# One engine for each bank of top-k candidates, constants loaded as listed work, and another order of the whole program

## The chip, the core and the metric

The kernel runs on one core of a Trainium2 chip. The core has a matmul engine (TensorE, PE in the profile, with its weight loads as PEld), a vector engine (VectorE, DVE), an activation engine (ScalarE, ACT), a general engine (GpSimd, POOL) and a queue engine (SyncE, SP), which here issues nearly all DMAs. Each engine works through its own list of instructions in order and waits on semaphores where it needs another's result. The metric is device time of one execution in microseconds (us); lower is better. Before the change the median of 3 runs is 329.95 us (326.61 to 335.99).

## What is computed

There are 4 batches of 12608 tokens of width 128, and 49 agents for each. The agents attend to the keys, which gives 49 agent values; every token's query then attends to the agents. On the result `x`, the 128 tokens of each batch with the highest gate score go through a two-layer network and are added back.

```python
a2k = softmax(scale * agents @ k.T)
agent_v = a2k @ v
x = softmax(scale * q @ agents.T) @ agent_v
scores = x @ w_gate
top = the 128 rows of each batch with the highest scores
out = x.copy()
out[top] += sigmoid(scores[top]) * (relu(x[top] @ w1) @ w2)
```

## The kernel before

A batch's tokens lie on 128 partitions in 99 columns, cut into 7 chunks (six of 15 columns, one of 9). For a batch the work has these steps, and the names in quotes are those of the work list.

- Keys: per chunk a load of 0.98 MB, two score products on PE ("S15", L343, 8 matmul instructions each), two turns on DVE (L349) and two maxima (L356). When all chunks are through, the maximum per agent is spread to all partitions ("mT", "mB", L385, and "mb", L388).
- Values: per chunk POOL subtracts the maximum ("X15", L398), ACT takes the exponential ("E15", L401), and PE multiplies with the chunk of v ("av", L413, two instructions for each column). After the last chunk the sums are gathered ("pw", L430) and scaled, and split in two half-precision parts, the weights `ws`.
- Queries: per chunk scores, maximum, subtraction (POOL, L485), exponential, split in two halves (L497, L498) and turns on PE ("fT", L513) with a copy out by DVE or ACT (L516).
- Gate scores ("pg", L537), then the reciprocal sums ("rates", L551 to L555).
- Results: for groups of up to 4 columns the products with `ws` ("po", L583, two instructions for each column), then an eviction that scales by the rates, on DVE in one instruction (L596) or on ACT in one for each column (L599), and a store of the chunk by SP (L604).
- Top-k (`topk`, L609): each partition's 8 best scores (L618) are spread by PE over two banks of PSUM, 4 candidates for each partition and bank ("all", L625). Every one of a partition's 8 candidates is compared with all 512 values of both banks, 16 comparisons of 512 columns for a batch. On each bank DVE does four (L633) and ACT does four (L638); the sums land in the tile `cnt` of that bank. Counts, places and indices follow on one more bank ("pc" L645, "at" L665, "p1" L672 to L675, "x8" L680, "pr" L681, "idx" L685 to L692).
- Experts: a gather of the chosen rows by POOL (L722), the attention of these rows again, the two layers (L810, L832) and a scatter (L840), for batches 0 to 2 together and for batch 3 alone.

The order is not left to the loops. `Work.op` only lists each piece of work with what it reads and writes; `Work.issue` (L209) then takes the 1302 pieces in the order of the table `ORDER` (L108), three characters each, the last bit of which says on which of two engines a piece runs (evictions, copies and relu have the choice). So a row of `ORDER` sets every engine's list, and SP's. Loads and result tiles share 8 buffers ("in"), scores share 28 ("s"), and the general PSUM banks are 6 ("b").

The reads and writes that a piece lists bound where the table may put it. The waits between engines are set below that, from the tiles and PSUM banks that instructions touch. A piece that compares a candidate lists the bank as read and its own column of `cnt` as written.

Three small loads stand outside the list, at the program's start, on ACT's queue: the agents, the constants `cst` (293 KB) and the gate weights (64 KB). `cst` is first read by "pw" of the first batch, apart from a conversion on DVE ("tri", L304).

Of the kernel before, what the change touches and what calls it, by code (L numbers as in the profile page):

```python
# [27 lines left out]
A = 49  # L28
# [12 lines left out]
ONACT = (4, 4, 4, 4)  # L41
# [5 lines left out]
TOP = 8  # L47
# [5 lines left out]
def const_layout(capacity):  # L53
    nst = max(1, -(-capacity // P))
    parts = {
        "sel": (2 * A),
        "steps": ROUNDS * (CANDS + 1),
        "offs": ROUNDS * CANDS,
        "jv": COLS,
        "slot": nst,  # L60
        "prow": 1,
        "tri": P,
        "srow": nst * P,
        "pcol": 1,
        "kk": TOP,
        "under": TOP * len(ONACT),
    }
# [4 lines left out]
    return at, pos, nst


def make_consts(capacity):
# [38 lines left out]
    "03001c09g05u09i0aw09k18216c15c0om0ra03q0361840aq0by0c003203405w16e16g01405y0601nw1ny08a03g03c04q0460oo15i"
    "09q09s0as1o00os0ou1o21o40480rc0re1860bu06204003e0rg15e04g03w16i0000oq0ri0ow04a04k18804i04s03y04u08c03m03o"
    "1o61o81oa0rk18a15k0bx18c0640661oc06815g15m03803a03i03k03s03u04204404c04e04m04o04w04y05019s1oi19y0520541a0"
    "1oe06a1og0s606c1ol0sc05606e05805a0rm15o0oy0ro08e0rq0rs05c0s806h0sa19u19w0se0pi05e0du0dx0pk0po0pm0pq1l615q"
    "05g1l81lc09m1le1a209o0fo0e20ps0qe0dg0dy0fr15s0e10do0di0dq1la0io0jg0ju0qk0qg0qi0fc0fe06i16k1a407o0ry0ru18e"
    "0s00p00sg0qm0e408g08m0iq0iu0rw08o1a60ji0iw0jm0jk0jw0jo0e60e90is0qo0j00iy0k00jy0k20k80ia0j20km0ea18w1pm15u"
    "08i08k0kg0js0jq0k40k60si0pu0pw0p20py09u15w0d80dc1601620p40kk0ki08q0df0sk0c40ii0im0j40j80ik0ja0jc0ku0kw0je"  # L120
    "08s0ka0ky0j60ic0fg15y0qq0q00fj07m0ko0fk0qs0fn16m0sm0ke0ie0ig0pa0pd0ks0p60p90l00le0fs14g0dk06k0q20b00l20c2"
    "1ps0l40kq0kc0l61pu0l80q60ay0d60so0sq0q51a80dn09w0su0da1po1pq1aa0lk0lu0me0mo0sw0qu19218y19019414m14o0ss0eg"
    "0ek0ej0ec0ef0ey1lg0en0f214i17417a0la0f51ag14k17c1961760fy1781pw17e0f00gq0gs1ai14q0mi0lo0lc0lw0lm0mg16o0m4"
    "0m61py1q016q0qw0ly0lg0li0lq0ls0m014s1980m80ms0ds0n20m216s16w0eu0mq0q816u0ex0g21ac0qy0g41ae0r116y0eo0eq19a"
    "10617g18g0ma0mc0mk0mm0my1li0n017i0mu0mw0n40n619c18i0g11lk19e0n80f60r20na0r50gc0f90gf0zs10e0g619k0g90nc0ne"
    "0ng0ni0nk0zu1qi1081qo1qq0zy0nm1lm14u19m0no1lo10c10g0tw0ok0pe1001021040zw10i10a18k0qa18o0r60pg0r80sy0s20tu"
    "0es0z00oi0z21qk0t00z41qm0z610k11c0ze10y0fa14w18q18m0fu0s40qc10s19g1lu0ty19i1lw0fx11k1qs10u10m0zm0gk0gn0zg"
    "0z811o10w10q11m0zo10o0zq0za0zc1qu14y1161500ua0x20u01qw0ud0x50zi1180zk11a11011e1540ue1m21m817k1520uh17m11g"
# [926 lines left out]
```

## Time and profile before

| | |
|---|---|
| median of 3 runs | 329.95 us (326.61 to 335.99) |
| the profiled execution | 330.46 us, its span 328.7 us |
| mean granted TensorE clock | 0.926 |
| busy: PE, DVE, ACT, POOL | 280.5, 218.2, 192.5, 143.3 us |
| moved by DMA | 106.70 MB, mean 325 GB/s |

The span runs from the first to the last instruction of the profiled execution, and its time lies 1.8 us above it. Busy time is a sum over the span, and the stages differ much: the first 50 us and the last 90 us do not look like the 150 us between. Matmuls overlap in PE's pipeline, and their ends are modelled, so that a fully busy PE isn't one at its peak; its clock is granted at one of two levels, 1.0 (2.4 GHz) or 0.5 (1.2 GHz) in the tables.

### The profile page before, as it was taken

What the parts mean: (1) busy time and instruction counts of PE and PEld (TensorE: products, weight loads), DVE (VectorE), ACT (ScalarE), POOL (GpSimd) and SP (SyncE); (2) the same over time, 40 slices, a digit from 0 to 9 for tenths busy, and PEclk for the clock granted to TensorE, in tenths of its full rate; (3) what the DMA queues carried; (4) which work ended last, traced back from release to release, by engine and by line L of the source; (5) the groups of instructions that cost most, each with busy time, mean ns of one, the idle gap of its engine ahead of it and who ended that gap; (6) DMA issues with size and microseconds to landing.
All of it is one profiled execution on the core that took longest, in us unless ns stands there. A gap on an engine that the chain in (4) does not pass through costs nothing. (4 is left out here: it accounts for less than half of the span.)

```text
span 328.7 us, 8664 instructions
## 1 busy us (share of the span) xinstructions
PE 280.5 (85%) x3524; PEld 194.7 (59%) x3524; DVE 218.2 (66%) x499; ACT 192.5 (59%) x446; POOL 143.3 (44%) x110
## 2 busy tenths in 40 slices
PE   0977868999999979999999798988466999599991
PEld 0322323496545647966356695656455999498791
DVE  0599995896799847069868748684096556577530
ACT  1063743725667638965487755865905567789540
POOL 0269488948835494941229640009505110001022
PEclk9999997999999979999999999999958556969997
DMA  8999999898998997999899999989793305655692
GB/s 282 425 426 416 425 420 406 346 422 352 370 342 330 378 421 251 348 410 417 291 352 367 381 310 395 383 328 403 271 394 134 129 10 197 252 242 224 278 381 78
DMA packets 18589, 106.70 MB, mean 325 GB/s; under 512 B 2544, under 2 KB 3824, under 8 KB 18544
## 3 DMA queue, kind: packets, MB, share of 16 engines
q1 hardware_dynamic: 17472, 105.07, 81.7%
q8 instruction: 30, 0.49, 0.6%
q0 software_dynamic: 256, 0.52, 0.5%
q10 hardware_dynamic: 816, 0.50, 0.5%
q14 instruction: 15, 0.12, 0.1%
HBM read 79.87 MB, written 26.21 MB: 323 GB/s over the span
## 5 line engine op out<-in xcount | busy, mean ns | idle before, releaser
L343 PE MATMUL b<-in,ag_sb 128*32 128x480 f32 (+1 forms) x896 | 100.2, 568 | 18.8 <-DMA in<-qT 10.2
L349 DVE STREAM_TRANSPOSE s<-b 128x480 f32<-128x480 f32 (+1 forms) x112 | 69.2, 635 | 27.3 <-PE b L343 26.1
L583 PE MATMUL b<-ws,s 98*128 98x128 f16 x792 | 66.1, 243 | 9.9 <-DVE in L596 8.0
L583 PEld LDWEIGHTS <-s 98*128 98x128 f16 x792 | 57.6, 111 | 24.3 <-issue 23.2
L343 PEld LDWEIGHTS b<-in,ag_sb 128*32 128x32 f32 x896 | 24.7, 112 | 62.6 <-issue 28.0
L599 ACT ACTIVATE in<-b,r 128x128 f32<-128x128 f32 x182 | 50.8, 403 | 17.1 <-PE b L583 10.8
L485 POOL TENSOR_TENSOR s<-s,qm 128x735 f32<-128x735 f32 (+1 forms) x28 | 37.9, 1369 | 46.5 <-DVE qm L483 33.0
L398 POOL TENSOR_TENSOR s<-s,mb 128x735 f32<-128x735 f32 (+1 forms) x28 | 46.7, 1700 | 25.2 <-DVE mb L388 25.2
L498 POOL TENSOR_TENSOR f<-s,f 128x735 f16<-128x735 f32 (+1 forms) x28 | 40.9, 1473 | 36.4 <-issue 21.6
L516 ACT COPY s<-b 98x1024 f16<-98x1024 f16 (+2 forms) x42 | 37.8, 918 | 30.4 <-PE b L513 29.1
L413 PE MATMUL v<-in,s 128*64 128x129 f32 x792 | 48.4, 279 | 3.6 <-DMA in<-va 2.4
L413 PEld LDWEIGHTS v<-in,s 128*64 128x64 f32 x792 | 45.6, 139 | 6.1 <-issue 3.5
L487 ACT ACTIVATE s<-s,lift 128x735 f32<-128x735 f32 (+1 forms) x28 | 24.5, 884 | 27.3 <-POOL s L485 27.2
L633 DVE SCALAR_TENSOR_TENSOR ge<-b,top,minus 128x512 bf16<-128x512 f32 x32 | 23.9, 746 | 24.4 <-ACT ga L638 22.9
L513 PEld LDWEIGHTS <-f 128*98 128x98 f16 x396 | 27.4, 133 | 17.5 <-issue 14.1
L513 PE MATMUL b<-idh,f 128*98 128x128 f16 x396 | 32.9, 232 | 2.4 <-DVE s L349 0.9
L356 DVE TENSOR_REDUCE mx<-b 128x1 f32<-128x480 f32 (+1 forms) x56 | 32.8, 606 | 2.3 <-PE b L343 0.9
L497 ACT CAST f<-s 128x735 f16<-128x735 f32 (+1 forms) x28 | 21.6, 786 | 13.2 <-POOL s L494 11.5
L638 ACT ACTIVATE ga<-b,top 128x512 bf16<-128x512 f32 x32 | 22.1, 691 | 10.0 <-DVE ge L633 8.2
L483 DVE TENSOR_REDUCE qm<-s 128x15 f32<-128x735 f32 (+1 forms) x28 | 23.5, 852 | 0.2
L401 ACT ACTIVATE s<-s 128x735 f32<-128x735 f32 (+1 forms) x28 | 21.0, 790 | 1.7 <-POOL s L398 1.7
L722 POOL DMA_INDIRECT xq<-q,idx x4 | 4.0, 1000 | 38.1 <-DVE idx L692 37.3
(132 smaller groups left out, 246.2 us busy)
## 6 DMA issues: line engine op xcount, KB each, us to landing
in<-va SPq DMA_DIRECT2D x24, 967.5 KB, 8.9
in<-qT SPq DMA_DIRECT2D x24, 960.0 KB, 10.0
in<-kT SPq DMA_DIRECT2D x24, 960.0 KB, 9.4
out<-in SPq DMA_DIRECT2D x24, 960.0 KB, 7.7
in<-va SPq DMA_DIRECT2D x4, 580.5 KB, 9.1
in<-qT SPq DMA_DIRECT2D x4, 576.0 KB, 7.2
in<-kT SPq DMA_DIRECT2D x4, 576.0 KB, 7.0
out<-in SPq DMA_DIRECT2D x4, 576.0 KB, 8.3
```

The costliest lines, as they stand in the source:

```text
L343: nc.tensor.matmul(ps()[32 * i:32 * i + 32, :w], ag_sb[:, b, 32 * h:32 * h + 32], x()[:, w * i:w * i + w], start=True, stop=True,)
L349: nc.vector.transpose(s()[:, :n, 32 * h:32 * h + 32], ps()[:, :w].rearrange("p (t c) -> p t c", c=32))
L356: op("V", f"M{n}", lambda _, h=h, ps=ps: nc.vector.tensor_reduce(top[:, c, h:h + 1], ps()[:, :w], axis=AX.X, op=ALU.max), r=[ps], w=[(f"mx ...
L398: op("G", f"X{n}", lambda _, sv=sv, n=n: nc.gpsimd.tensor_tensor(sv(), sv(), d["mb"].unsqueeze(1).broadcast_to([P, n, A]), op=ALU.subtract ...
L413: nc.tensor.matmul(av()[o:o + AP_, :C + 1], s()[:, t], x3[:, t], start=(j < 2), stop=(j >= COLS - 2))
L485: op("G", f"qx{n}", lambda _: nc.gpsimd.tensor_tensor(sv(), sv(), wide, op=ALU.subtract), r=[f"qm{b}{c}"], w=[s])
L487: op("A", f"qe{n}", lambda _: nc.scalar.activation(sv(), sv(), AF.Exp, scale=SCALE, bias=lift), w=[s])
L498: op("G", f"ql{n}", lambda _: nc.gpsimd.tensor_tensor(f()[:, :n, A:], sv(), f()[:, :n, :A], op=ALU.subtract), r=[s, (f, 0)], w=[(f, 1)])
L513: nc.tensor.transpose(wide_pt()[:R, P * (t - lo):P * (t - lo) + P], f()[:, t, :], idh)
L516: (nc.vector.tensor_copy if e == "V" else nc.scalar.copy)(flat(ft()).bitcast(F16)[:R, P * lo:P * hi], wide_pt()[:R, :P * (hi - lo)])
L583: nc.tensor.matmul(p3()[:, t - lo], d["tile", c](t), ws[:, b, i, :C], start=(i == 0), stop=(i == 1))
L599: nc.scalar.activation(o4[:, t - lo], p3()[:, t - lo], AF.Copy, scale=d["r"][:, j0 + t:j0 + t + 1])
```

## The change

On the first bank of candidates DVE now does all 8 comparisons, on the second ACT all 8; before it was 4 and 4 on both. The threshold `under` loses its per-batch columns. The copy "x8" goes from ACT into DVE's "p1". The loads of `cst` and of the gate weights become pieces of the list, on SP, with the reads of them listed. And the whole table `ORDER` is another one, with 1300 pieces.

```diff
-ONACT = (4, 4, 4, 4)
...
-        "under": TOP * len(ONACT),
+        "under": TOP,
...
-    under = np.full((len(ONACT), TOP), capacity - 0.25, np.float32)
-    for b, n in enumerate(ONACT):
-        under[b, TOP - n:] -= 512.0
-    c[:, slice(*at["under"])] = under.reshape(1, -1)
+    c[:, slice(*at["under"])] = capacity - 0.25 - 256.0
...
-    "0c60nq0nw0ny0ns0nu0o00o20cc0t20t80ta0t40t60tc0te0tg0o40c80ca0ce0cg08u0900920ci0ck0ti08w0o606m06s06u06o06q"
+    "0ca0cc0cg0ce0ci0t40t60ck0cm0co0cq0cs0cu0t80cw0cy0d00ns0nu0ny0ta0nw0o00tc0te0tg0ti0tk0tm0a20a80oo0ou0ow0aa"
...
-    nc.scalar.dma_start(cst, consts)
     wg_sb = own("wg_sb", [P, C])
-    nc.scalar.dma_start(wg_sb, wgb)
+    op("S", "dma308", lambda _: nc.sync.dma_start(cst, consts), w=["cst"])
+    op("S", "dma66", lambda _: nc.sync.dma_start(wg_sb, wgb), w=["wg"])
...
-        side8 = TOP - ONACT[b]
...
             for k in range(TOP):
-                if k < side8:
+                if h == 0:
                     op("V", "ge", lambda _, h=h, k=k, bk=bk: nc.vector.scalar_tensor_tensor(
...
         def marks(_):
             nc.vector.tensor_copy(bs, at())
+            nc.vector.tensor_copy(x[:, TOP:TOP + 1], at()[:, 0:1])
...
-        op("V", "p1", marks, r=[pc], w=[f"p1{b}", f"fl{b}"])
-        op("A", "x8", lambda _: nc.scalar.copy(x[:, TOP:TOP + 1], at()[:, 0:1]), r=[pc], w=[(f"x{b}", 1)])
+        op("V", "p1", marks, r=[pc], w=[f"p1{b}", f"fl{b}", (f"x{b}", 1)])
```

What the two tables make of the engines' lists is shown at two places. The first is the stretch behind the last batch's key maximum, where the comparisons of batches 1 and 2 stand before, and those of batch 2 after. In a row, `c11` is the sum tile of bank 1 of batch 1 (`c02`: bank 0 of batch 2), the `b` behind the arrow is the PSUM bank that is read, and a wait names the engine whose semaphore is waited on. DVE before, from the last batch's `mb` on:

```order
L388 COPY mb3_236<-b4_107 128x49 [waits PE_49]
L633 SCALAR_TENSOR_TENSOR ge_147,c02_224<-b0_103,top2_222,minus2_133 128x512
L516 COPY s9_81<-b5_108 98x1024 [waits PE_49]
L349 STREAM_TRANSPOSE s25_97<-b2_105 128x15x32 [waits PE_49]
L633 SCALAR_TENSOR_TENSOR ge_147,c02_224<-b0_103,top2_222,minus2_133 128x512 [waits DVE_49]
L349 STREAM_TRANSPOSE s25_97<-b4_107 128x15x32 [waits PE_49]
L596 TENSOR_TENSOR in0_64<-b5_108,r1_194 128x384 [waits DMAHW0_49,PE_49]
L633 SCALAR_TENSOR_TENSOR ge_147,c11_198<-b2_105,top1_195,minus2_133 128x512 [waits DVE_49,PE_49,Activation_49]
L633 SCALAR_TENSOR_TENSOR ge_147,c01_197<-b3_106,top1_195,minus2_133 128x512 [waits DVE_49,Activation_49]
L633 SCALAR_TENSOR_TENSOR ge_147,c02_224<-b0_103,top2_222,minus2_133 128x512 [waits DVE_49]
L596 TENSOR_TENSOR in0_64<-b5_108,r1_194 128x512 [waits DMAHW6_49,PE_49]
```

and ACT before, in the same stretch (L401 are the exponentials "E15" of the last batch):

```order
L638 ACTIVATE ga_148,c11_198<-b2_105,top1_195 128x512 [waits Activation_49]
L401 ACTIVATE s23_95<-s23_95 128x15x49 [waits Pool_49]
L680 CAST x0_172<-b1_104 128x1
L638 ACTIVATE ga_148,c12_225<-b4_107,top2_222 128x512 [waits DVE_49,PE_49,Activation_49]
L638 ACTIVATE ga_148,c11_198<-b2_105,top1_195 128x512 [waits Activation_49]
L638 ACTIVATE ga_148,c02_224<-b0_103,top2_222 128x512 [waits Activation_49]
L401 ACTIVATE s14_86<-s14_86 128x15x49 [waits Pool_49]
L401 ACTIVATE s10_82<-s10_82 128x15x49 [waits Pool_49]
L401 ACTIVATE s6_78<-s6_78 128x15x49 [waits Pool_49]
L638 ACTIVATE ga_148,c11_198<-b2_105,top1_195 128x512 [waits Activation_49]
L401 ACTIVATE s5_77<-s5_77 128x9x49 [waits Pool_49]
```

DVE's comparisons on `c11` and `c01` wait for ACT, which in its turn has comparisons on the same two tiles spread between the exponentials; three DVE rows behind the first of them stands an eviction of results (L596). DVE after, behind the same `mb`:

```order
L628 SCALAR_TENSOR_TENSOR ge_145,c02_222<-b1_104,top2_220,minus2_131 128x512
L680 SCALAR_TENSOR_TENSOR e21_201<-b3_106,cst_115 128x1 [waits PE_49]
L683 SCALAR_TENSOR_TENSOR e21_201<-cst_115,e21_201,b3_106 128x8 [waits DVE_49]
L687 SCALAR_TENSOR_TENSOR idx1_202<-b3_106,e21_201 128x1 [waits DVE_49]
L628 SCALAR_TENSOR_TENSOR ge_145,c02_222<-b1_104,top2_220,minus2_131 128x512
L628 SCALAR_TENSOR_TENSOR ge_145,c02_222<-b1_104,top2_220,minus2_131 128x512 [waits DVE_49] x2
L592 TENSOR_TENSOR in2_66<-b4_107,r2_219 128x128 [waits DMAHW4_49,DMAHW1_49,PE_49]
L628 SCALAR_TENSOR_TENSOR ge_145,c02_222<-b1_104,top2_220,minus2_131 128x512 [waits DVE_49] x2
L614 MAX_INDEX at82_221<-top2_220,scs_142 128x8
L479 TENSOR_REDUCE qm_3_4_243<-s17_89 128x15
L628 SCALAR_TENSOR_TENSOR ge_145,c02_222<-b1_104,top2_220,minus2_131 128x512 [waits DVE_49]
L592 TENSOR_TENSOR in1_65<-b2_105,r2_219 128x512 [waits DMAHW6_49,PE_49]
```

and ACT after:

```order
L397 ACTIVATE s0_72<-s0_72 128x15x49 [waits Pool_49]
L397 ACTIVATE s7_79<-s7_79 128x15x49 [waits Pool_49]
L633 ACTIVATE ga_146,c12_223<-b5_108,top2_220 128x512 [waits DVE_49,PE_49]
L633 ACTIVATE ga_146,c12_223<-b5_108,top2_220 128x512 [waits Activation_49] x2
L397 ACTIVATE s16_88<-s16_88 128x15x49 [waits Pool_49]
L633 ACTIVATE ga_146,c12_223<-b5_108,top2_220 128x512 [waits Activation_49]
L397 ACTIVATE s23_95<-s23_95 128x15x49 [waits Pool_49]
L633 ACTIVATE ga_146,c12_223<-b5_108,top2_220 128x512 [waits Activation_49] x4
L648 COPY b1_104<-cst_115 128x128 [waits DVE_49,PE_49]
```

There each tile (`c02`, `c12`) is on one engine alone, and no comparison waits for the other engine but the first of ACT's, which also waits for PE's spread; the comparisons of batches 0 and 1 have left this stretch for earlier ones.

The second place is the start. ACT before, its first five rows:

```order
L265 DMA ag_sb_113<-agT 128x4x64
L267 DMA cst_115<-consts 128x586
L269 DMA wg_sb_117<-wgb 128x128
L487 ACT_TABLE_LOAD
L487 ACTIVATE s1_73<-s1_73,lift_129 128x9x49 [waits Pool_49]
```

ACT after:

```order
L261 DMA ag_sb_113<-agT 128x4x64
L483 ACT_TABLE_LOAD
L483 ACTIVATE s0_72<-s0_72,lift_127 128x9x49 [waits Pool_49]
L487 ACTIVATE qm_0_6_164<-qm_0_6_164,eps_129 128x9 [waits DVE_49]
L493 CAST f0_100<-s0_72 128x9x49 [waits Pool_49]
```

The load of the constants has left ACT's queue. It stands in SP's list behind the loads of batch 0's values, 40 rows in, and SP issues it when the loads ahead have their buffers:

```order
L326 DMA in6_70<-va 128x1935 [waits DMAHW7_49,PE_49]
L326 DMA in7_71<-qT 128x1920 [waits PE_49]
L264 DMA cst_115<-consts 128x562 [waits DMAHW0_49]
L326 DMA in0_64<-qT 128x1920 [waits DMAHW1_49,PE_49]
L326 DMA in4_68<-qT 128x1920 [waits DMAHW2_49,PE_49]
```

The pieces of choice are split otherwise too: evictions of results are 39 on DVE and 69 on ACT before, 48 and 60 after; copies of turned tiles ("fT") are 14 and 42 before, 20 and 36 after. The two large loads of expert weights (0.46 MB each) stand right behind the last load of values before; after, `w1` stands behind three stores of results that follow those values, and `w2` behind six.

## Rows read from the trace of the kernel before

**Rows 1.** The page, the granted clock in 40 slices of the span.

```profile
PEclk9999997999999979999999999999958556969997
```

**Rows 2.** Busy time by stage: start and end, length, engines (instructions), clock, DMA.

```profile
0.00:51.00 51.00, 34.11 (x321) 12.03 (x321) 38.77 (x75) 20.26 (x30) 28.60 (x28) 1.00 0.98 400
51.00:76.70 25.70, 25.70 (x334) 16.75 (x334) 17.94 (x28) 11.31 (x15) 20.42 (x14) 0.93 0.98 391
76.70:221.90 145.20, 136.10 (x1913) 88.97 (x1909) 104.88 (x224) 97.53 (x193) 70.09 (x50) 0.99 0.94 356
221.90:254.80 32.90, 21.64 (x283) 18.77 (x282) 18.04 (x49) 17.84 (x43) 16.11 (x10) 0.87 0.79 299
254.80:300.70 45.90, 41.92 (x502) 40.45 (x503) 28.32 (x91) 33.92 (x125) 3.25 (x4) 0.69 0.40 159
300.70:328.70 28.00, 21.03 (x179) 17.72 (x178) 10.26 (x33) 11.62 (x42) 4.87 (x5) 0.93 0.66 265
```

**Rows 3.** Waits: engine and line, waited for: total us, times, longest.

```profile
DVE ge L633 <- ACT ga L638: 22.9, 8, 11.1
ACT ga L638 <- DVE ge L633: 8.2, 5, 3.5
```

**Rows 4.** Timeline from 221 us: start, length, engine, work, [idle before <-releaser].

```profile
221.89 0.43 PE L385 MATMUL b<-dg,ones_f 2*128 2x64 f32 x2
...
222.65 11.64 POOL L398 TENSOR_TENSOR s<-s,mb 128x735 f32<-128x735 f32 x7 [21.40 <-DVE mb L388]
...
228.53 3.53 PE L413 MATMUL v<-in,s 128*64 128x129 f32 x60 [1.02 <-ACT s L401]
...
237.34 0.75 DVE L633 SCALAR_TENSOR_TENSOR ge<-b,top,minus 128x512 bf16<-128x512 f32 x1 [11.07 <-ACT ga L638]
...
240.68 1.01 PE L583 MATMUL b<-ws,s 98*128 98x128 f16 x8 [6.48 <-DVE in L596]
...
253.36 0.17 PE L681 MATMUL b<-x,p 128*128 128x10 bf16 x1 [2.63 <-DVE flags L675]
...
254.83 0.75 PE L430 MATMUL b<-avs,cst 128*98 128x129 f32 x2 [0.43 <-DVE e L685]
```

**Rows 5.** Windows as in rows 2, first and last of four in a row.

```profile
254.00:260.00 6.00, 5.57 (x45) 5.24 (x43) 3.72 (x16) 3.95 (x14) 0.00 (x0) 0.50 0.28 110
...
272.00:275.00 3.00, 3.00 (x27) 3.00 (x26) 2.79 (x10) 2.90 (x12) 0.00 (x0) 0.50 0.09 22
```

**Rows 6.** Timeline, PE's work in short bursts at full clock.

```profile
200.89 1.82 PE L343 MATMUL b<-in,ag_sb 128*32 128x480 f32 x16 [0.82 <-DMA in<-kT]
...
203.46 0.94 PE L537 MATMUL x<-ws,s 98*128 98x3 f16 x30
...
204.25 0.63 PE L513 MATMUL b<-idh,f 128*98 128x128 f16 x8
...
208.36 1.08 PE L583 MATMUL b<-ws,s 98*128 98x128 f16 x16
...
218.81 1.14 PE L625 MATMUL b<-idf,top 128*128 128x128 f32 x8
...
303.97 1.45 PE L810 MATMUL b<-xT,s 128*128 128x384 f32 x4
```

**Rows 7.** Timeline, the end of the last batch's top-k.

```profile
283.13 0.75 DVE L633 SCALAR_TENSOR_TENSOR ge<-b,top,minus 128x512 bf16<-128x512 f32 x1 [4.59 <-ACT ga L638]
...
300.36 0.33 ACT L680 CAST x<-b 128x1 bf16<-128x1 f32 x1
...
300.74 0.17 PE L681 MATMUL b<-x,p 128*128 128x10 bf16 x1
```

**Rows 8.** Groups of instructions by line and form: count, busy us, mean ns.

```profile
L596 DVE TENSOR_TENSOR in<-b,r 128x512 f32<-128x512 f32 x22 | 14.9, 684 | 1.5 <-PE b L583 1.3
```

**Rows 9.** Timeline, the start.

```profile
8.02 12.29 PE L343 MATMUL b<-in,ag_sb 128*32 128x480 f32 x104 [8.02 <-DMA in<-qT]
```

**Rows 10.** DMA issues: bytes, us from issue to landing.

```profile
cst<-consts ACTq DMA_DIRECT2D x1, 293.0 KB, 7.5
```

More of the change, by code (lines that the diff above doesn't have):

```diff
@@ L114 @@
[L114 to L128, printed above, removed]
@@ new lines @@
+    "0ao00k15c08007w0bm0700bo0bq08207y00s00m07200u15i15e0rq09c0rs0ru0740p20p408400o15k0bs00q07600w15g09e15m05m"
+    "0s00rw05o0d60bu0ry0d80s20p60qu09g0bw00y05q0100pc01201401605s05u0p80by0c101a07807a05w0aq0c20pe0q00pa0as01c"
+    "01k0240ji02601e01m01o01i0180jq01g0c509i01q02i0060au0ay0js02a0ju01s01y0qw0b002802k02o02m02q01w02u01u02c022"
+    "05y0q207c0aw07e08607g0qy15o15q0j40s802002e07i00e02g00i00g07m00800c0sa0q809k07o09m00a02w02y0300sc0se032034"
+    "09o0880360qa02s07l08a0sg04u0021680iq16a0r00q40r416e16c0si06008c0iy0is16g0r316i0j215s15u03g03q08e0iu08g0sk"
@@ new lines @@
+    "03a0jw0380r609u0j609w0ko03k0ka0ic15w15z06206403i09q03c03e0iw0660j00q70kq0jy0k20ku0k40k80jk0ja09s0680kw0l0"
+    "0j803m03o0jc0ky0jo0ks0jg0k60jm0je0ie0kc0ki0ik0ii0io0kg0km0l20ke0k00kk03u04404e04y04o18000003s0sm04a04004c"
+    "08i0so0sq0sw04203w03y04604804g0ig0sy1600l408k16k16m04k08m08q0ss0l60l804m16o04w16208o0im08t0la0lm06a06c0n0"
+    "04i04q04s0500521860540su0lc0lw16q05605818218418806e06i06k05a17417617817a17c05c06g0m60le05e05i05k05g14g14m"
+    "14i19s19y19u14o1a014k0ma18w0lq0m00lg0fa0ea0fs0ed0lo0fu0fk0fm14q19w08w0e60b20b40e90fd16s0f60dy0f90e10c80e2"
@@ L147 @@
+    "1to1ba1ry1v61v01vc1xc1bc1wi1cq1dq1wg0xg1d81tq1s01se1vw1vu1vq1vm1vs1xm1xo1vi1vk1xa1xe1xy1xi1xq1xl1y11xt1vo"
+    "1tg1ya1tk1y21v41v21va1v81ve1ti1yd1y51tn1vy1w01w21bi1ts1tu1rg1w41y61u21ss1bl1tw1bq1rj1y91w61w81wa1rs1sk1sg"
+    "1b41sv1yy1u41sm1aw1sj1ay1xu1b71ro1rq1so1sq1xx1ru1t21rk1ta1tc1ty1u61rn1u81yg1z01ua1t61u11z21t41z41z61uc1yk"
+    "1sy1z81za1zc1ze1ug1uo1zg1xg1t91t11zi1ui1yi1ur1zm1zs1zw1zy1zk1b81rw1sw1ue1ye1yo1yq1zu1yu2021yw1te1us1ym1zo"
+    "1zq2001ys204206"
 )
@@ L305, in triangles @@
         nc.vector.tensor_tensor(tri_i, cs("tri"), idf, op=ALU.add)
-    op("V", "tri", triangles, w=["tri"])
+    op("V", "tri", triangles, r=["cst"], w=["tri"])
     st = [{} for _ in range(B)]
@@ L430, in values_end @@
         op("P", "pw", lambda _: nc.tensor.matmul(pw()[:R, :C + 1], cs("sel"), a, start=True, stop=True),
-           r=[f"a{b % 2}"], w=[pw])
+           r=[f"a{b % 2}", "cst"], w=[pw])
         def scaled(_):
@@ L655, in rows_in @@
             nc.scalar.copy(x[:, :TOP], at8)
-        op("A", "srow", rows_in, r=[f"at8{b}"], w=[pc, (f"x{b}", 0)])
+        op("A", "srow", rows_in, r=[f"at8{b}", "cst"], w=[pc, (f"x{b}", 0)])
         op("V", "mk", lambda _: nc.vector.scalar_tensor_tensor(
-            m[:, :TOP], pc()[:, :TOP], -0.5, cs("under")[:, TOP * b:TOP * b + TOP],
+            m[:, :TOP], pc()[:, :TOP], -0.5, cs("under"),
             op0=ALU.mult, op1=ALU.is_lt, accum_out=m[:, TOP:],
```

46 lines of the change are left out of this document (23 added, 23 removed).

## Prediction

> **What bounds the kernel now.** I read the granted clock first [rows 1]: it is 1.0 or near it through three quarters of the span and about half of that in several slices of the last quarter. Then I cut the span at four places of the program [rows 2]: the key maximum of batch 0 (51.0 us), the gathering of batch 0's values (76.7), the key maximum of batch 3 (221.9) and the gathering of batch 3's values (254.8), and last at that batch's "pr" (300.7). The reader is to see three regimes. Up to 76.7 us the DMA engines are busy 0.98 of the time: the loads set the pace. From 76.7 to 221.9 PE is busy 136.1 of 145.2 us at a clock of 0.99: PE sets the pace, with little idle time. In the last three stages, 106.8 us, neither does. Between 221.9 and 254.8 PE is busy 21.6 of 32.9 us, and between 254.8 and 300.7 it is busy 41.9 of 45.9, but at a mean clock of 0.69.
>
> The waits name a cause. DVE's comparisons wait 22.9 us in total for ACT's, and ACT's 8.2 us for DVE's [rows 3], though neither needs the other's result: they meet on one bank and one sum tile. The longest is in that stage [rows 4]: a comparison on DVE starts at 237.34 after 11.07 us of idle time, and behind it in DVE's list stands an eviction that PE needs for a free bank, so PE starts at 240.68 after 6.48 us idle. At 253.36 PE has been idle again for 2.63 us, and then it works from 254 to 275 us almost without a break at a clock of 0.50 [rows 5].
>
> **The price of PE's work.** At full clock [rows 6]: a score matmul 1.82/16 = 0.114 us, a result matmul 1.08/16 = 0.0675, a turn 0.63/8 = 0.079, a gate score 0.94/30 = 0.031, a spread 1.14/8 = 0.1425, an up product of the experts 1.45/4 = 0.36; a value product 3.53/60 = 0.059 [rows 4]. I count a batch's 99 columns and the pieces of both orders in each stage.
>
> *Stage four* (key maximum of batch 3 to "pw"). Before: 16 score matmuls 1.8, 198 value products 11.7, results of 19 columns 38 x 0.0675 = 2.6, 16 spreads 2.3, the rest 1.5; in all 20 us of work in 32.9 us. After: 24 score matmuls 2.7, values 11.7, results of 35 columns 4.7, 8 spreads 1.1, the rest 1; in all 21 us. The comparisons of batches 0 and 1 have left the stage, so DVE has 8 instead of 16 there and ACT 8 instead of 16, and none waits for the other engine. The next latest thing is POOL's subtraction, seven chunks in 11.64 us, with which two other POOL pieces of some 1.5 us now mix: 14.6 us, and after it an exponential and the last value products. That lies under PE's 21 us. I take 24 us, 3 above the work, since PE must start on other things while the first chunk passes POOL and ACT. Bounds: 21 (nothing waits) and 32.9 (another wait takes the place of this one). Gain 9, between 0 and 12.
>
> *Stage five* ("pw" to "pr" of batch 3). Before: results of 156 columns 21.1, turns 2.4, gate scores 3.1, spreads 2.3, experts and small ones 5; in all 34 us of work in 45.9. After: 103 columns 13.9, 38 turns 3.0, gate scores 3.1, spreads 2.3, 14 up products 5.1, experts and small ones 5; in all 32 us. The difference of 12 us before is nearly all clock: 21 us at 0.50 [rows 5] give back 10. What triggered it were the idle spells of stage four, which this change takes away; here too a comparison had waited 4.59 us for ACT [rows 7]. I take 36: the 32, and 4 for the chain through "rates", eight comparisons side by side on each engine, "pc" and "pr". Bounds: 32, and 46 where the clock falls as before. Gain 10, between 0 and 14.
>
> Here a rule can be weighed. The rows show the clock at 0.50 for 21 us while PE is busy 20.6 of them. The Trainium skill, TensorE: Matmul & The Clock Gate, Part 1, says that the throttled state is the default and that activity releases it. By that page a PE as busy as this would have got its clock back early in those 21 us and the half-clock spell would be worth little, so that the stage would come out near 34 with or without the idle spells; the trace does not agree, and I keep the measured 10 us.
>
> *Stage six* ("pr" to the end), 28.0 us. PE's work there falls by about a microsecond, and it ends in the same chain of expert, last stores and scatters. I take 28; bounds 26 and 31, the upper one if `w2`, now behind six stores, comes late.
>
> *Stages one to three.* By the key maximum of batch 3 the new order has given PE 10 more columns of results (1.35 us), 8 more spreads (1.1) and some small matmuls (0.6), and 8 fewer score matmuls (0.9): +2 us. By the gathering of batch 0 it has asked for 35.8 MB where the old one had 27.6 (counts of loads times their size): at 398 GB/s, between the rates of rows 2, that is 90 us against 69, while PE has 22.6 us more work done (15 score pieces of 8 matmuls, 106 turns). The old order was there at 76.7, so the new one is due near 76.7 + 22.6 = 99, and the loads with their lag stay just under it. At the start the first matmul waits until 8.02 us for a chunk [rows 9], the second in SP's list, with `cst` moving beside it; now only the small first chunk is needed. I take -3 there, and -1 for the three stages together; bounds -6 (the opening keeps all of it) and +10 (loads and DVE stop each other in the opening, as the second rival works out).
>
> **Edits with a price near nothing.** The nine evictions and six copies moved to DVE cost it 9 x 0.684 [rows 8] = 6 us and some 4 for the copies, over a span in which DVE is busy 218 of 329 us; cover is its idle time, and in the opening it has least. "x8" in "p1" saves the 0.33 us of ACT and its queue before the last "pr" [rows 7], inside stage five. The smaller `under` is nothing. The late `cst` adds a wait: "pw" of batch 0 stands in PE's list in order, and if the constants are not there all PE stands. They took 7.5 us to land [rows 10]; between their place and "pw" PE has some 11 us of work, so I take 0, bounds 0 and 5.
>
> **The sum.** Span 328.7 - 1 - 9 - 10 - 0 = 308.7; the profiled time was 1.8 above its span, so 310.5. That execution (330.46) stands 0.5 above the median of 329.95. I forecast **310 us**, own range 300 to 319.
>
> **The rivals.**
> - *The clock falls again.* The comparisons no longer wait, but PE still idles a little before "pw", as at 253.36, and stage five runs at half clock as before: 328.7 - 1 - 9 + 1.8 = **320**. For it: a spell of 2.6 us was enough. Against it: that spell came from a DVE list which was 11 us late. 0.20.
> - *The opening gives it back.* By batch 0's gathering DVE was busy 38.8 + 17.9 = 56.7 us of 76.7 [rows 2], with 94 pieces; in the new order it has 133 by that point. At the same mean and the same busy share that is 56.7 x 133/94 = 80 us of work and 108 us of time, where PE alone gave 99: 9 to 10 us later, and the gain of 1 is gone. The tail keeps its gain: **321**. Against it: the DVE share of 0.76 in the first 51 us holds the 8 us before the first matmul [rows 9], and it may rise. 0.17.
> - *The waits were cover.* POOL's subtractions and the exponentials end stage four where they ended it before, so the lost comparisons free nothing, and idle time and clock stay: **327**. Against it: POOL was through at 234.3, and "pw" came 20 us later. 0.10.
> - *Slower: half clock through the tail.* Stages five and six are many small half-precision matmuls, and rows 5 show that such work may stay at 0.50 although PE is busy. Half clock stretches a result burst by at most 2; at 1.7 for PE's work, stage five takes 58 instead of 36 and stage six 42 instead of 28, which gives 310 + 36 = **346**. The gain of 20 us is eaten up when 20/0.7 = 29 us of work, 49 us on the clock, run at half speed; stage five had 45.9 x 0.31 x 2 = 28 us of it [rows 2]. Against it: stage six, where the same work is mixed with the experts', had a mean clock of 0.93 [rows 2], and the new order moves up products into stage five. 0.08.
>
> The forecast keeps 0.45. A measurement of this kernel tells 2% from no change, so faster means under 323.4 and slower above 336.5. Faster: the forecast's 0.45, three quarters of the first rival (0.15), more than half of the second (0.10), together 0.70. Slower: the last rival and a little of the third, 0.09. Within 2%: the rest, 0.21. The range reaches from 299, where stages four and five reach their lower bounds and the opening keeps half of its gain, to 328, which takes in the third rival; some 0.07 lies below and 0.12 above.
>
> **What would show it.** Right: no row in which a comparison of one engine waits for the other's; "pw" of batch 3 some 24 us behind its key maximum; a clock of 0.9 or more between "pw" and "pr"; the first matmul near 5 us. Wrong: PE idle before batch 0's "pw" with the constants as releaser; a long idle row of PE in stage four with POOL or ACT as releaser; slices of 5 in the clock line over more than a tenth of the span.

## The result and the profile after

The changed kernel takes 295.88 us (median of 4 runs, 293.68 to 300.7) against 331.45 (4 runs, 326.61 to 335.99) of the kernel before: a ratio of 0.899, interval 0.885 to 0.913. (Ratios, here and below, compare only those runs of a kernel that lie within 1.5% of its fastest.) The forecast of 310 had the direction, but the time lies below its range of 300 to 319, and below the 299 that the prediction names at another place too. The profiled execution took 295.63 us with a span of 293.6.

First the page: PE's busy time and the clock granted to it in 40 slices, and three groups of instructions (count | busy us, mean ns | idle before, releaser).

```profile
PE 262.5 (89%) x3524; PEld 179.6 (61%) x3524; DVE 224.1 (76%) x516; ACT 180.5 (61%) x405; POOL 143.2 (49%) x110
...
PEclk9999999999999999999999999999789999999997
...
L579 PE MATMUL b<-ws,s 98*128 98x128 f16 x792 | 55.6, 219 | 1.6 <-DVE in L592 1.6
...
L628 DVE SCALAR_TENSOR_TENSOR ge<-b,top,minus 128x512 bf16<-128x512 f32 x32 | 23.9, 748 | 1.6 <-PE b L620 0.8
...
L633 ACT ACTIVATE ga<-b,top 128x512 bf16<-128x512 f32 x32 | 22.0, 689 | 0.8 <-PE b L620 0.3
```

Of the run of fives and sixes in [rows 1] nothing is left. The comparisons on DVE idle for 1.6 us in total and those on ACT for 0.8, where they had waited 22.9 and 8.2 for each other [rows 3].

Then the same six stages as in [rows 2], cut at the same four places of the program and at "pr" of batch 3 (start and end, length, busy time of PE, its weight loads, DVE, ACT and POOL, clock, DMA share, GB/s).

```profile
0.00:61.40 61.40, 49.02 (x476) 17.74 (x476) 50.43 (x95) 31.92 (x44) 41.73 (x37) 1.00 0.99 404
61.40:92.70 31.30, 31.10 (x415) 20.22 (x415) 24.80 (x48) 17.89 (x24) 25.95 (x17) 1.00 1.02 418
92.70:218.40 125.70, 114.86 (x1706) 81.70 (x1702) 93.70 (x215) 81.18 (x186) 49.94 (x37) 0.97 0.96 364
218.40:240.30 21.90, 20.92 (x314) 17.65 (x312) 17.23 (x52) 16.30 (x34) 18.02 (x12) 1.00 0.90 337
240.30:268.20 27.90, 27.77 (x410) 24.65 (x409) 25.81 (x73) 24.13 (x86) 2.71 (x3) 1.00 0.74 284
268.20:293.60 25.40, 18.80 (x217) 17.60 (x214) 12.12 (x36) 9.05 (x33) 4.89 (x5) 0.94 0.75 302
```

Batch 0's gathering comes at 92.7 instead of 76.7, yet batch 3's key maximum at 218.4 instead of 221.9: 3.5 us gained over stages one to three. Stage four falls from 32.9 to 21.9 us, stage five from 45.9 to 27.9, stage six from 28.0 to 25.4. The sum is 3.5 + 11.0 + 18.0 + 2.6 = 35.1 us of span, and stage five is half of it. There PE is busy 27.77 of 27.9 us at a clock of 1.00; before, it was busy 41.92 of 45.9 at 0.69.

The timeline of PE in that stretch has the rows that mark the stages, and the run of forty results that the experiments come back to.

```profile
218.44 0.43 PE L381 MATMUL b<-dg,ones_f 2*128 2x64 f32 x2
...
240.29 0.43 PE L426 MATMUL b<-avs,cst 128*98 128x129 f32 x2
...
251.37 2.45 PE L579 MATMUL b<-ws,s 98*128 98x128 f16 x40
...
268.24 0.17 PE L676 MATMUL b<-x,p 128*128 128x10 bf16 x1
```

None of them carries an idle time in brackets; before, "pr" of an earlier batch came after 2.63 us of it and a result burst after 6.48 [rows 4].

### The profile page after: what moved, and what is told of

Same layout as the page of the kernel before. It is cut to its first block, busy times and chain, and to the rows that moved or that the text cites. A ratio compares the mean times of both kernels' runs of the same rounds, so it can differ in the third digit from the quotient of the medians.

```text
span 293.6 us, 8629 instructions
## 1 busy us (share of the span) xinstructions
PE 262.5 (89%) x3524; PEld 179.6 (61%) x3524; DVE 224.1 (76%) x516; ACT 180.5 (61%) x405; POOL 143.2 (49%) x110
## 4 chain that ended last, share of the span: by engine, by line
PE 45%; DMA 30%; DVE 17%; ACT 4%; issue 2%; POOL 0%; POOLq 0%; SPq 0%; DVEq 0%; ACTq 0%
PE b L339 15%; PE v L409 12%; DMA in<-qT 12%; DMA out<-in 9%; PE b L579 8%; DMA in<-va 6%; DVE s L345 6%; PE b L509 5%; DVE mx L352 3%; DVE qm L479 3%; DMA in<-kT 3%; ACT in L595 2%; ACT ga L633 2%; DMA ag_sb<-agT 1%; PE x L533 1%
## 5 line engine op out<-in xcount | busy, mean ns | idle before, releaser
L345 DVE STREAM_TRANSPOSE s<-b 128x480 f32<-128x480 f32 (+1 forms) x112 | 67.7, 630 | 13.5 <-PE b L339 12.6
L339 PEld LDWEIGHTS b<-in,ag_sb 128*32 128x32 f32 x896 | 26.0, 112 | 64.4 <-issue 28.8
L579 PE MATMUL b<-ws,s 98*128 98x128 f16 x792 | 55.6, 219 | 1.6 <-DVE in L592 1.6
L512 ACT COPY s<-b 98x1024 f16<-98x1024 f16 (+2 forms) x36 | 32.3, 920 | 33.3 <-PE b L509 33.3
L579 PEld LDWEIGHTS <-s 98*128 98x128 f16 x792 | 47.8, 98 | 6.8 <-issue 5.5
L595 ACT ACTIVATE in<-b,r 128x128 f32<-128x128 f32 x149 | 40.9, 386 | 12.5 <-PE b L579 7.6
L409 PEld LDWEIGHTS v<-in,s 128*64 128x64 f32 x792 | 44.3, 136 | 4.1 <-DMA in<-va 1.2
L352 DVE TENSOR_REDUCE mx<-b 128x1 f32<-128x480 f32 (+1 forms) x56 | 32.9, 608 | 7.4 <-PE b L339 7.4
L509 PEld LDWEIGHTS <-f 128*98 128x98 f16 x396 | 25.5, 126 | 21.0 <-issue 14.6
L509 PE MATMUL b<-idh,f 128*98 128x128 f16 x396 | 30.7, 224 | 1.7 <-POOL f L494 1.4
L592 DVE TENSOR_TENSOR in<-b,r 128x512 f32<-128x512 f32 (+2 forms) x40 | 24.8, 645 | 5.1 <-DMA out<-in 3.2
L397 ACT ACTIVATE s<-s 128x735 f32<-128x735 f32 (+1 forms) x28 | 21.9, 790 | 5.4 <-POOL s L394 5.4
```

Source lines behind the costliest of these rows:

```text
L339: nc.tensor.matmul(ps()[32 * i:32 * i + 32, :w], ag_sb[:, b, 32 * h:32 * h + 32], x()[:, w * i:w * i + w], start=True, stop=True,)
L345: nc.vector.transpose(s()[:, :n, 32 * h:32 * h + 32], ps()[:, :w].rearrange("p (t c) -> p t c", c=32))
L352: op("V", f"M{n}", lambda _, h=h, ps=ps: nc.vector.tensor_reduce(top[:, c, h:h + 1], ps()[:, :w], axis=AX.X, op=ALU.max), r=[ps], w=[(f"mx ...
L409: nc.tensor.matmul(av()[o:o + AP_, :C + 1], s()[:, t], x3[:, t], start=(j < 2), stop=(j >= COLS - 2))
L509: nc.tensor.transpose(wide_pt()[:R, P * (t - lo):P * (t - lo) + P], f()[:, t, :], idh)
L512: (nc.vector.tensor_copy if e == "V" else nc.scalar.copy)(flat(ft()).bitcast(F16)[:R, P * lo:P * hi], wide_pt()[:R, :P * (hi - lo)])
```

## The experiments

The change has two large parts, the split of the comparisons and the new order. Four kernels take the parts singly; the rest ask what moves the clock of stage five.

**The split alone, and the order alone.** In the order of before, each bank to one engine; and in the new order, the old split:

```
-        under[b, TOP - n:] -= 512.0
+        under[b] -= 256.0
...
-                if k < side8:
+                if h == 0:
```
```
-    c[:, slice(*at["under"])] = capacity - 0.25 - 256.0
+    c[:, slice(*at["under"])] = capacity - 0.25
+    c[:, at["under"][0] + 4:at["under"][1]] -= 512.0
...
-                if h == 0:
+                if k < 4:
```

> The order table of before, with only the comparisons split by bank (DVE all 8 on the first bank, ACT all 8 on the second; the threshold to match). Theory S, the gain comes from the waits between the two engines: the 22.9 and 8.2 us of waits are gone, the stage from the last key maximum to pw takes 24 us and not 33, the clock between pw and pr is 0.9 or more, and the time is 305 to 313. Rival O, the gain comes from the new order (comparisons of batches 0 and 1 earlier, loads and evictions placed otherwise): the old order stays near 325, since DVE and ACT still have all the comparisons of batches 1 and 2 behind the last key maximum.

> The changed kernel with the old split (4 candidates on DVE and 4 on ACT, on both banks) under the new order table. Theory S: comparisons wait for the other engine again, some 20 us of waits in all, PE idles and the clock falls behind the last key maximum; 310 to 320. Rival O: the waits return but lie in stretches where DVE and ACT have room; within 3% of the changed kernel, 296 to 304.

The split alone gave 319.53 us, ratio 0.967 [0.960, 0.975]; the order alone 317.69, 0.964 [0.956, 0.972]. That is 10 and 12 us; together they give 34. Stages four, five and six of the split alone in windows, then the start of its stage five in the timeline, and two 3-us windows behind that:

```profile
222.60:242.80 20.20, 18.60 (x283) 16.47 (x283) 18.22 (x50) 15.57 (x37) 13.14 (x8) 1.00 0.99 369
242.80:290.70 47.90, 41.10 (x506) 39.74 (x503) 28.71 (x90) 37.34 (x134) 6.28 (x6) 0.71 0.52 210
290.70:318.30 27.60, 21.03 (x179) 17.72 (x178) 10.25 (x33) 11.62 (x42) 4.88 (x5) 0.92 0.67 268
```
```profile
245.13 0.69 ACT L638 ACTIVATE ga<-b,top 128x512 bf16<-128x512 f32 x1
...
245.81 2.35 ACT L599 ACTIVATE in<-b,r 128x128 f32<-128x128 f32 x8
245.96 1.86 PE L583 MATMUL b<-ws,s 98*128 98x128 f16 x16 [2.72 <-ACT ga L638]
...
250.53 0.96 PE L645 MATMUL b<-c,idf 128*128 128x8 f32 x4
...
254.73 0.97 PE L537 MATMUL x<-ws,s 98*128 98x3 f16 x31
```
```profile
248.00:251.00 3.00, 3.00 (x24) 3.00 (x22) 1.51 (x5) 2.25 (x9) 0.00 (x0) 0.50 0.99 396
...
260.00:263.00 3.00, 3.00 (x53) 3.00 (x51) 2.49 (x12) 2.64 (x12) 1.52 (x2) 0.50 0.15 44
```

The split by itself brings stage four to 20.2 us at full clock, the whole gain there, and nothing of stage five. So the step "idle time of stage four lowers the clock of stage five" falls as it stood: that idle time is gone and the half clock is not. A new wait has come in its place. A bank that belongs to ACT alone puts its comparisons in one lump in ACT's list of the old order. PE's next results wait 2.72 us for the last of them, as the row's releaser says; the eviction L599 behind the lump starts only when that wait ends. Then PE works at 0.50 until about 266, without a pause.

The order alone, stages four and five, and two 3-us windows with one row of PE from the middle of its stage five:

```profile
224.90:254.40 29.50, 22.39 (x313) 19.66 (x312) 17.89 (x52) 16.21 (x34) 17.52 (x12) 0.88 0.79 283
254.40:289.30 34.90, 31.19 (x411) 27.08 (x410) 26.12 (x73) 25.05 (x86) 3.17 (x4) 0.91 0.63 243
```
```profile
262.00:265.00 3.00, 3.00 (x75) 2.99 (x72) 2.52 (x6) 1.13 (x5) 0.00 (x0) 1.00 0.45 189
265.00:268.00 3.00, 3.00 (x51) 3.00 (x48) 2.73 (x12) 2.47 (x11) 0.00 (x0) 0.63 0.36 144
```
```profile
265.48 4.03 PE L580 MATMUL b<-ws,s 98*128 98x128 f16 x40
```

The two engines still wait for each other (ACT's comparisons 25.6 us in total for DVE's, DVE's 14.0 for ACT's), and stage four takes 29.5 us. Yet stage five is at 34.9 us and a clock of 0.91, where the split alone, without these waits, has 47.9 and 0.71. So it is the order, and not the end of the waits, that brings most of the clock of stage five back. One more thing is seen in the windows: behind the gate scores the clock fell to 0.50 for some 3 us although PE had not paused since 237; the forty results took 4.03 us. The same row of work stood at 1.00 in the changed kernel.

**The lump taken out.** The same kernel, with four of the eight comparisons on batch 2's second bank left out and their counts zero. That sends the tail into its repair of a batch, so only the time up to "pr" (283.1 us), not the 497 us of the whole, can be read:

```
+                nc.vector.memset(cnt[1], 0.0)
...
+                    less = b == 2 and k in (0, 4, 5, 6)
-                    op("A", "ga", lambda _, h=h, k=k, bk=bk: nc.scalar.activation(
+                    op("A", "ga", lambda _, h=h, k=k, bk=bk, less=less: less or nc.scalar.activation(
...
```

> The order of before with whole banks to one engine, and four of the eight comparisons of ACT on batch 2's second bank left out (their counts are set to zero, so which candidates are taken differs; the work behind is the same). In the run with all of them PE waited 2.72 us at 243 for these comparisons (the evictions stand behind them in ACT's list), and the clock then stood at 0.50 from 247 to 266 with PE busy throughout. Theory, a pause of PE at the head of stage five starts the half clock: the pause goes, stage five is at 1.00 up to some 265, and falls from 47.9 to 35 to 39 us; time 307 to 311 us. Rival, the old row of small products holds the clock down by itself: the pause goes and nothing else, stage five 45 us, time 316 to 318. Rival, the comparisons cost what they take: stage five 44, time 315, the clock as before.

Windows of the stretch after the place where the wait had been, and two later rows of its PE:

```profile
245.00:248.00 3.00, 3.00 (x64) 3.00 (x62) 2.36 (x9) 2.89 (x13) 1.15 (x2) 1.00 1.04 420
248.00:251.00 3.00, 2.76 (x78) 2.69 (x75) 2.43 (x10) 1.74 (x9) 0.21 (x1) 1.00 0.60 237
251.00:254.00 3.00, 2.70 (x69) 2.56 (x66) 1.43 (x9) 2.73 (x11) 1.90 (x2) 1.00 0.07 18
...
257.00:260.00 3.00, 3.00 (x21) 2.94 (x22) 1.55 (x4) 2.55 (x9) 0.00 (x0) 0.50 0.57 238
```
```profile
256.86 2.05 PE L630 MATMUL b<-idf,top 128*128 128x128 f32 x8 [0.60 <-DVE top L621]
...
268.35 2.17 PE L583 MATMUL b<-ws,s 98*128 98x128 f16 x22 [2.21 <-ACT ga L644]
```

PE's same list of work, from results to gate scores, ran at 1.00 for 12 us where it had run at 0.50: the pause had started that spell. The old order has more of them. After several short ones around 251 to 257 the clock is down until about 261, and after the next lump (2.21 us for ACT) again. Stage five came to 40.8 us, not the 35 to 39 expected: its first half was mended, and the second has lumps of its own.

**A pause put into the changed kernel.** Added operations on DVE ahead of the copy that "pw" of batch 3 needs (four, then nine):

```
+        def gathered(_):
+            if b == B - 1:
+                nc.vector.tensor_copy(ge[:, 0:1], av()[:, :1])
+                for i in range(4):
+                    nc.vector.scalar_tensor_tensor(
+                        ge, ge, eps, minus2.broadcast_to([P, 512]), op0=ALU.is_gt, op1=ALU.mult
+                    )
             nc.vector.tensor_copy(a, av()[:, :C + 1])
...
```

> The changed kernel with 4 more DVE instructions of some 0.7 us ahead of the copy that pw of the last batch waits for, so that PE idles some 2.5 us there. Clock theory (an idle spell like the one before pw in the kernel before brings a spell of half clock): the clock between pw and pr falls well under 0.9, and the time grows by the delay and 5 to 10 us more, 303 to 308. Rival (the spell alone does nothing): the delay of 2.5 us at most, 296 to 299, clock 1.0.

> The same with 9 instructions, PE idle some 6 us, as long as the longest idle spell of the kernel before in its last third. Clock theory: delay 6 us and 5 to 10 us more for half clock, 307 to 312. Rival: the delay alone, 300 to 303, clock near 1.0 behind it.

They took 299.85 and 302.72 us, about the delay more (pauses of 3.10 and 7.29 us) and less than the 303 to 308 and 307 to 312 of the clock theory. Yet the clock did fall. With nine, PE stood still for 7.29 us, and this is what followed (the row behind the pause, then windows in which the pause, the fall and the return are seen):

```profile
244.47 0.72 PE L435 MATMUL b<-avs,cst 128*98 128x129 f32 x2 [7.29 <-DVE e L689]
```
```profile
238.00:241.00 3.00, 0.00 (x0) 0.00 (x0) 2.87 (x4) 0.36 (x2) 0.00 (x0) 1.00 1.02 417
241.00:244.00 3.00, 0.00 (x0) 0.00 (x0) 2.88 (x4) 0.00 (x0) 0.00 (x0) 0.72 0.82 335
244.00:247.00 3.00, 2.53 (x21) 2.50 (x22) 2.07 (x13) 0.92 (x4) 1.86 (x2) 0.50 0.12 40
247.00:250.00 3.00, 3.00 (x37) 3.00 (x36) 1.91 (x4) 1.56 (x6) 0.66 (x1) 0.65 0.01 3
250.00:253.00 3.00, 3.00 (x65) 3.00 (x63) 2.46 (x9) 2.33 (x11) 0.19 (x1) 1.00 0.02 5
```

The pause lowered the clock, but it was back by 249, and stage five was only 2.2 us longer (30.1). The same kind of pause had cost the old order 20 us at half clock. So a pause is only half of the cause. Behind this one stood half-precision results and turns of 128 columns and little else; in the split alone, from 248 on, products of 8 and of 3 columns (L645 and L537 above) stand among the results.

**The pause moved ahead of, and behind, the short products.** In the changed kernel the gate scores (three columns each) run from 246 to 251.5. Eight DVE operations ahead of a copy before them; eight reciprocals in the rates behind them:

```
+                if (b, c, lo) == (3, 5, 0):
+                    for i in range(8):
+                        nc.vector.scalar_tensor_tensor(
...
```
```
+            if b == B - 1:
+                for i in range(8):
+                    nc.vector.reciprocal(ge.bitcast(F32)[:, :COLS], r)
```

> The new kernel with eight added operations on DVE ahead of the eviction of batch 3's chunk 5 (about 5 us, at 243), so that PE runs out of banks just ahead of the run of three-column products. Theory, any pause of PE ahead of small f16 products starts a half clock that lasts some 20 us: stage five 27.9 plus 4 of pause plus 8 to 10 = 40 to 42 us, time 307 to 310. Rival, the new order's row brings the clock back within some 5 us wherever the pause is, as behind the pauses of 2.5 and 6 us ahead of pw: stage five 33 to 35, time 300 to 303.

> The new kernel with eight added reciprocals on DVE (about 6 us) in the forming of the last batch's rates, behind the run of three-column products, so that PE runs out of banks at some 253 us. With the pause ahead of those products the clock stood at 0.50 for 16.6 us; with pauses ahead of pw, where rows of 128 columns follow, for 3 to 5 us. Theory, what PE does behind the pause sets how long the half level lasts: rows of 128 columns and the experts' f32 products follow, so it is back within 5 us; stage five 27.9 plus 4 to 6 of pause plus 2 = 34 to 36 us, time 302 to 305. Rival, it depends on how late in the stage the pause falls: 0.50 for 15 us or more, stage five 40, time 308.

Ahead of them: 307.36 us (its two runs took 309.61 and 305.11), stage five 39.2. The rows of PE:

```profile
253.00 1.01 PE L584 MATMUL b<-ws,s 98*128 98x128 f16 x8 [5.53 <-DVE s L517]
...
256.48 0.80 PE L538 MATMUL x<-ws,s 98*128 98x3 f16 x23
...
262.64 1.41 PE L538 MATMUL x<-ws,s 98*128 98x3 f16 x46
263.91 4.22 PE L584 MATMUL b<-ws,s 98*128 98x128 f16 x40
...
268.30 1.06 PE L625 MATMUL b<-idf,top 128*128 128x128 f32 x8
```

The clock stood at 0.50 through the gate scores and came back while the forty results ran: they took 4.22 us, against 2.45 in the changed kernel. Behind them: 305.22 us, stage five 38.8. After a pause of 6.20 us the clock was at 0.50 until about 269, some 9 us of PE's work. That is neither the 5 us of the one theory nor the 15 of the other. The work behind this pause is spreads, results and the experts' products, all of 128 columns, the spreads and the experts' in f32 (four bytes a value); the clock is back while the first products of 384 columns run (the row at 268.13):

```profile
259.58 2.05 PE L623 MATMUL b<-idf,top 128*128 128x128 f32 x8 [6.20 <-DVE top L616]
...
265.59 2.74 PE L582 MATMUL b<-ws,s 98*128 98x128 f16 x24
268.13 1.33 PE L808 MATMUL b<-xT,s 128*128 128x384 f32 x2
269.39 0.93 PE L783 MATMUL b<-wfs,xq 49*128 49x129 f32 x6
```

So the number of columns by itself does not order these spells: behind the pause ahead of "pw" products of 128 columns stood too, and there the clock was back within 5 us.

**Short products without a pause, and with one.** Eight f32 products of 8 columns ahead of each of seven result banks (the profile counts 112 for them); alone, and with the pause of nine operations:

```
+                if (b, c, lo) in SMALL:
+                    for i in range(8):
+                        nc.tensor.matmul(p3()[:, 0, :8], idf, idf[:, :8], start=True, stop=True)
```

> The new kernel with eight f32 products of 8 columns added ahead of each of seven banks of results from the start of stage five on (56 more matmuls; the results are written over them). Theory, a row of short products alone does not lower the clock while PE has no pause: clock 1.00 in stage five, stage five longer by 56 times 0.05 to 0.1 = 3 to 6 us, time 299 to 302. Rival, short products lower it by themselves: half clock in stage five, stage five 38 or more, time 306 or more.

> The pause of 6 us ahead of pw of the last batch (nine added operations on DVE, which alone gave 302.7 us, with the clock at 0.50 for 5 us) together with the 56 short f32 products behind it. Theory, behind a pause the short products keep the clock at the half level: 0.50 for 10 us or more, and the time is 4 to 7 us above the sum of the two alone. Rival, they do not: the sum, that is 302.7 and what the short products alone add (3 to 6), 306 to 309, and the clock back within some 5 us.

Alone they made the time 323.82 us, far over the 299 to 302 expected. Much of that is the price of the products themselves, which the expectation had too low. The first row of sixteen ran at full clock, the second at half; the seven rows together make 21 us:

```profile
238.29 1.85 PE L580 MATMUL b<-idf 128*128 128x8 f32 x16
...
247.57 3.53 PE L580 MATMUL b<-idf 128*128 128x8 f32 x16
```

So the time decides nothing, and the clock has to be read. The windows of that kernel:

```profile
239.00:242.00 3.00, 3.00 (x34) 3.00 (x33) 0.79 (x4) 1.45 (x6) 2.17 (x2) 1.00 1.02 416
242.00:245.00 3.00, 3.00 (x31) 3.00 (x31) 1.22 (x2) 0.00 (x0) 0.00 (x0) 0.77 0.84 340
245.00:248.00 3.00, 3.00 (x24) 3.00 (x24) 0.19 (x1) 1.04 (x4) 0.00 (x0) 0.50 0.07 20
...
278.00:281.00 3.00, 3.00 (x22) 2.99 (x21) 1.64 (x3) 2.21 (x9) 0.00 (x0) 0.50 0.82 261
281.00:284.00 3.00, 3.00 (x31) 2.75 (x31) 2.53 (x8) 2.05 (x6) 0.00 (x0) 0.97 1.02 304
```

PE has no pause there at all, and the clock falls to 0.50 among the short products and stays there until the forty results and the spreads behind them are through. My theory, that they need a pause to do harm, falls. With the pause the time was 335.19, that is 4.5 above the sum of the two alone (295.88 + 6.84 + 27.94 = 330.66), within the 4 to 7 expected.

**The price of a result, the chain, the constants.** Three smaller terms: every result of the last batch computed twice, the copy "x8" back on ACT, the constants back at the start of ACT's queue.

```
-                    for i in range(2):
+                    for i in (0, 1, 0, 1)[2 * (b < B - 1):]:
```
```
-            nc.vector.tensor_copy(x[:, TOP:TOP + 1], at()[:, 0:1])
+            nc.scalar.copy(x[:, TOP:TOP + 1], at()[:, 0:1])
```
```
+    nc.scalar.dma_start(cst, consts)
+    nc.scalar.dma_start(wg_sb, wgb)
...
```

> The changed kernel with every result product of the last batch done twice (198 more matmuls, same values), all of them behind the last pw. Theory P, PE's own work fills the stages behind pw and I overpriced it, since a short burst's row includes the wait for its last matmul: at 0.057 us each 11 us more, most of it in the stage from pw on. With the price of the prediction (0.0675): 13 us more. Rival, another engine or the stores bound these stages: under 5 us more.

> The changed kernel with the copy x8 on ACT again, at the same place of the list. The copy was priced as part of the chain to the last pr, which was taken to bind the stage; if it binds, 1 us or more longer (297 or more); if PE's work hides that chain, no change (295 to 297).

> The changed kernel with the constants and the gate weights loaded at the program's start on ACT's queue again. If the late load costs nothing and saves nothing: 295 to 297, first matmul up to 1 us later since 0.35 MB more move beside the first chunk. If the late load was worth something: 298 or more. If PE waited for it at the first pw: under 294.

The doubled results (198 more matmuls) gave 305.61 us in the profiled execution, and stages five and six together 64.45 us against 53.3: 11.1/198 = 0.056 us for one. The clock stayed at 1.00 in stage five, with results of 128 columns the only addition. "x8" on ACT: 295.97, ratio 0.898 [0.890, 0.905], no difference. The early constants: 297.53 us in the profiled execution, ratio 0.912 [0.903, 0.922], which overlaps with the interval of the changed kernel; the first matmul started at 5.04 us, so beside the small first chunk the constants hold nothing up. One of this kernel's four executions took 451.21 us; the record does not show why.

## Why the prediction was wrong

**Stage five is the term that failed.** It was put at 36 us with bounds of 32 and 46, and came to 27.9, below the lower bound. The 36 were 32 us of PE's work and 4 us of idle time; measured are 27.77 and 0.1. These two pieces, 4.2 and 3.9 us, are the whole error of the term, and 8 of the 15 us by which the span missed (308.7 - 293.6).
- *The price of the work.* Prices came from short bursts [rows 6], in which the delay of the last product is shared by few: 1.08/16 = 0.0675 us for a result. The run of forty gives 2.45/40 = 0.061, and the doubling 0.056 for each added one. For the 206 results of the stage that is 2.4 us of the 4.2; the other kinds were priced from bursts in the same way and were not measured singly. The Trainium skill, TensorE: Matmul & The Clock Gate, "Wait — 56ns, not 53.3ns?", gives 55.6 ns from start to start at 128 columns and full clock; the doubling agrees with that, and the bursts do not.
- *The idle time.* PE idled 4.0 us of the stage before and 0.1 after. The sum took the price of the work as the floor and then put 4 us on it for the chain through comparisons, "pc" and "pr". That chain is covered by other work of PE: putting one step of it, "x8", back on ACT changed nothing.
- *The clock hid the first.* Full clock was forecast and came. But for the kernel before the sum gave back 10 us for 21 us at half clock [rows 5], and these rows end before a second spell, which follows the comparison of [rows 7]:

```profile
287.00:290.00 3.00, 3.00 (x27) 3.00 (x24) 1.78 (x6) 1.95 (x8) 0.00 (x0) 0.50 0.50 205
```

The row of the whole stage has 0.69 over 45.9 us [rows 2], which is 45.9 x 0.31 x 2 = 28 us at half clock, and up to 14 us to give back. The last rival used these 28 us; the sum did not. With 34 us of work and 10 of clock the stage before seemed explained; with 14 of clock and 4.0 of idle time only some 28 of its 45.9 us are left for the work, and the price would have been seen to be too high.

**The mechanism behind that term was half right.** The prediction said that idle spells of stage four lower the clock of stage five, and that taking out the waits between the engines cures it. The split alone takes out these waits and most of stage four's pauses, and the clock of stage five is 0.71; the order alone has the waits, and it is 0.91. So the full clock was forecast rightly for a reason that does not hold, and that part was luck: the prediction gave the new order no share in it. The signs that it named for being right (no waits between comparisons, "pw" 24 us behind the key maximum, a clock over 0.9, the first matmul near 5 us) came in, and could not tell the two reasons apart.

What holds of it is the kind of cause: each pause of 2.21 to 7.29 us that PE had in stages four and five of these runs was followed by 0.50, and with the pause of the split alone taken out the same work ran at 1.00. What the prediction lacked is the second half. How long 0.50 lasted behind a pause differed with the work that followed, counted from PE's next start: some 5 us with half-precision results and turns, 9 with f32 spreads and experts' products among the results, 15 to 23 with gate scores and other short products among them. Which property of that work decides was not isolated. Nor is a pause needed: the added f32 products took the clock down with none, and so did the row with the gate scores in the order alone. The new order has neither a lump of comparisons that results wait for nor a pause next to the gate scores. This would explain why the two parts together give 34 us and singly 10 and 12: either part alone leaves PE with pauses in its last stages. That the interaction is wholly the clock was not isolated.

**The rule that was weighed.** The prediction kept the trace's 20.6 busy us at 0.50 against a rule. The runs bear the trace out and sharpen it: in the kernel with short products PE was busy 3.00 of every 3.00 us and lost its clock, so equally full rows stand at 1.00 and at 0.50, and busy time as the profile counts it does not tell which. The Trainium skill, TensorE: Matmul & The Clock Gate, Part 1, has activity as what releases the throttle; these rows agree with it only if activity is not read as that busy time.

**The other terms.**
- *Stage four*, put at 24, came to 21.9; the priced work, 21, was nearly right, and the 3 us on top for PE starting on other things was not needed. The waits went as forecast, and POOL did not become the bound.
- *Stages one to three*, put at -1, gave -3.5. Batch 0's gathering came at 92.7, where 99 was expected and the second rival had 108 (15 score pieces and 106 turns are 22.0 us by the prediction's own prices, not 22.6, which still rounds to 99): DVE was busy 50.4 of the first 61.4 us, 0.82 against 0.76. The first matmul started at 5.16 us as said, but with the constants back it started at 5.04: the 3 us come from the small first chunk, and no share of them is due to `cst`.
- *Stage six*, put at 28, came to 25.4, where 26 was the lower bound. With DMA at 0.75 of the time against 0.66 it holds the same kind of work at nearly the same clock (0.94 and 0.93); PE's busy time fell by 2.2 us, not by one. Why was not tried further.
- *The edits at nothing* were at nothing, as far as "x8" and the constants show.

The rival at 346 named a danger that the runs bear out: such work does stay at 0.50 while PE is busy. In the changed kernel's profiled execution nothing set it off in the last stages.

## What to carry to other kernels

Price a stage that runs at a reduced clock by its own mean over the whole stage, and price PE's work by what one more instruction adds in a long run, not by a short burst; then put nothing on top for a chain unless a row shows PE waiting for it. When a stage before a change is explained as work, clock and idle time, take each of the three from its own row, or one error hides another. When an order is found for a tuned kernel, read the clock behind each pause of PE, since the same few microseconds of idle time had very different prices here by the place where they fell. Two changes of which each moves a wait somewhere else can be worth far more together than the sum, so a part that gives little alone is not yet refuted.

## What the hardware showed

- Among added f32 products of 8 columns the clock fell without any pause of PE: 1.00 before 242 us, 0.50 from 245 to 281, PE busy throughout. Each such instruction took 1.85/16 = 0.116 us at full clock and 3.53/16 = 0.22 at half.
- At half clock the run of forty results took 4.22 us against 2.45, but 46 gate scores of three columns 1.41 against 1.37 (the kernel with the pause ahead of them and the changed kernel): work of so few columns hardly shows the clock.
- Beyond its own length, a pause of 7.29 us ahead of "pw" made stage five 2.2 us longer, one of 6.20 us ahead of the spreads 4.7, and one of 5.53 us ahead of the gate scores 5.8.
